# A written-out opening in another order: blocks 0, 8 and 12 loaded ahead of the first weight slab, single roots for blocks 0 and 4, and the second chunk's first unit in token halves

## The chip, the core and the metric

The kernel runs on one core of one Trainium2 chip. The core has TensorE (PE, matmuls; its weight loads are shown as PEld), VectorE (DVE), ScalarE (ACT), GpSimd (POOL) and a sync engine (SP) that issues the DMAs. The metric is the device time of one execution in microseconds; less is better. A profiled execution gives a span (first to last instruction) and the start and length of every instruction in it. Times inside the program are us from the span's start.

## What is computed

```python
xn = _layernorm(x)                                   # x: 2048 tokens x 448, float32
A  = irfft2(rfft2(xn) * (w_r + 1j * w_i))            # a filter in the frequency domain
g  = xn @ W_gate; u = xn @ W_up                      # 448 -> 1792
B  = (where(g > 0, g, 0) * u) @ W_down               # 1792 -> 448
return x + A + B
```

Every matrix product is made from float16 halves (a high part and the rest) so that float32 accuracy is kept: three matmuls in place of one.

## The kernel before

The 2048 tokens are 16 *blocks* of 128 tokens. Four blocks form a *chunk*: chunk 0 has blocks 0, 4, 8 and 12, the next one in the work's order, chunk 2, has blocks 2, 6, 10 and 14. A block is loaded, its mean and variance taken, normalized, split into a high and a low half (tile `tt`), and transposed; the transposed chunk is the tile `T` (512 token columns, 128 for each block). In the opening, chunk 0 is transposed by TensorE through PSUM and copied out; chunk 2 by DMA transposes from SP.

The gate and up weights come as 14 *slabs* (`W0` to `W13`), each with a gate half `g0` and an up half `g1` of 256 KB. The scale of a half comes from its squares (ACT), a sum over all partitions (POOL) and two bit steps on DVE; then its high half is made by one pass (ACT) and its low half by another (DVE). A *unit* is one slab on one chunk: ten matmuls per half into a PSUM bank, with some closing matmuls on half the rows (line L764), and then ACT and DVE passes (relu, product, split). After five slabs the down product of the group begins (line L834). The spectral part runs on DVE and in between on TensorE.

All engines run their instructions in program order. For the body a planner sets that order from costs. The opening, up to the first units of chunk 2, is instead a list of piece names, `OPENING`, read from left to right: each name issues its instructions at that place on each engine, so two pieces of different engines keep only their own engine's order. The names used here:

- `lxN`, `lyN`: load block N for normalizing, for the residual. The packet `lx4` is larger: it also holds the 128x128 identity that TensorE's transposes need as their second operand.
- `stN`: statistics of a block (BN_STATS and BN_AGGR on DVE). `sqA`, `rsA` (B, C): reciprocal root on ACT and four small DVE steps, for two or four blocks at once. In the change also `sqN`, `rsN`, `nmN` for one block, the last step (bias) apart.
- `xnN` on DVE, `axN` on ACT: the normalized block in float32. `hiN` on ACT from the input, `hxN` on ACT from the normalized block, `vhN` on DVE: its high half. `loN` (DVE): its low half. `cpN` (POOL): two small copies.
- `tpAN`, `tpBN`: three and five TensorE transposes of a block. `vevAN`, `aevAN` (and B): their copy out of PSUM by DVE or by ACT.
- `lw`: the next weight half; `lwdF`: a down slab. `wsqWFgG` squares, `parWF` POOL's sum, `wscWF` scale, `whiWFgG` the high half on ACT (`vwWFgG`: on DVE), `wloWFgG` the low half on DVE.
- `warm`, `kwN`, `warmN`: matmuls without a result, on a zeroed tile (line L1098).
- `hhGH`, `lhGH`, `hlGH`: slab 0's matmuls on chunk 0, for half G of the weights and token half H (256 columns). `ahGH`, `bhGH`, `chGH`: the same for slab 1. `hqGB`, `lqGB`, `kqGB`: on a single block B (0: block 0, 1: block 4).
- `guFgG`: a later slab on chunk 0; `hpF`: closing matmuls; `gzFgG`: slab F on chunk 2; `gyFgGhH`, `gxFgGhH`: the same on token half H. `re`, `tm`, `gh`, `gl` (`rz`, `tz`, `hz`, `lz`): the passes behind a unit. `dmN`: DMA transpose of a block. `n0`: four small copies of rows of chunk 0. `lfd`: load of the table `fd_t`.

SP's loads use eight semaphores in turn, so a load is issued only when the one eight places ahead has landed. The weight buffer `wst` has eight places.

Of the kernel before, what the change touches and what calls it, by code (L numbers as in the profile page):

```python
# [10 lines left out]
F32 = mybir.dt.float32  # L11
# [22 lines left out]
tpB12 wsqW3g0 vevB8 wloW1g0 ah10 wsqW3g1 vevB12 ah01 parW2 ah11 lwd2 wloW1g1 wscW2 bh00 hl11 hl01 lx14 whiW2g0
bh01 hp0 ch10 whiW2g1 lw st2 bh11 st6 re0 wloW2g0 bh10 wsqW4g1 ch00 ch11 tm0 gu2g0 parW3 wscW3 st14 wsqW4g0
whiW3g0 wloW2g1 ch01 ly0 parW4 wscW4 whiW3g1 wloW3g1 lw wsqW5g1 lx10 whiW4g0 wloW3g0 gh0 re1 st10 gu2g1 tm1 hp2
sqC rsC wsqW5g0 xn6 gu3g0 re2 parW5 wscW5 whiW5g0 tm2 wloW4g0 xn10 xn14 hx14 lwd4 hx6 lo6 hi10 whiW5g1 lo10
gu4g0 hx2 wloW5g0 whiW4g1 cp14 xn2 wdq0 gl0 cp10 gu3g1 wloW4g1 lo14 lwd3 wdq4 wdq2 cp2 re3 tm3 cp6 wloW5g1 gh1
gu4g1 gh2 wdq3 ly12 lo2 hp4 wdq1 wdp wdsc wdh4 dm10 gl1 re4 ly8 wdh3 gl2 gu5g1 tm4 gh4 dm14 gl4 dm6 gu5g0 dm2
re5 lfd gz0g0 wdl3 gz0g1 tm5 hp6 gh3 gl3 rz0 gh5 wdl4 gl5 wdh1 wdl1 wdh2 wdl2 n0 wdh0 wdl0 gz1g0 tz0 gz1g1 rz1  # L40
hz0 tz1 hz1 lz0 lz1
"""
# [102 lines left out]
def tile_gfnet_reglu(ctx: ExitStack, tc: tile.TileContext, x, xr, xi, wgu, wd, wf, c_fd, c_fm, c_im, c_row, c_id,  # L145
# [104 lines left out]
    mv = {}  # L250

    def ln_stats(q, j):
        n2 = q + 4 * j
        st = ft([128, 6], F32, "bst", 2)
        V.bn_stats(st, xr_t[n2])
        if j == 0:
            mv[q] = ft([128, 4, 2], F32, "mv", 2)
        V.bn_aggr(mv[q][:, j, :], st)

    rst = {}  # L260

    def ln_sd(q, js=(0, 1, 2, 3)):
        w = ft([128, 4, 4], F32, "rs", 3)
        n = len(js)
        rst[q, js[0]] = w[:, :, 0:n], mv[q][:, js[0]:js[-1] + 1, :]
        A.activation(w[:, 0, 0:n], rst[q, js[0]][1][:, :, 1], AF.Abs_reciprocal_sqrt, bias=eps)

    def ln_rstd(q, js=(0, 1, 2, 3), bias=False):
        w, m = rst[q, js[0]]
        r0, t, r, nm = (w[:, i] for i in range(4))  # L270
        V.scalar_tensor_tensor(t, m[:, :, 1], 1e-5, r0, op0=OP.add, op1=OP.mult)
        V.scalar_tensor_tensor(t, t, -0.5 * 2048, r0, op0=OP.mult, op1=OP.mult)
# [25 lines left out]

    def ln_hi(n2, fused=False):
        new_tt(n2)  # L300
        o = tt[n2].rearrange("p a b -> p (a b)")[:, 0:D]
        r, nm, _ = rst[n2 % 4, n2 // 4]
        if fused:
            A.activation(o, xr_t[n2], AF.Identity, scale=r, bias=nm)  # L304
        else:
            A.activation(o, xn[n2], AF.Copy)
# [789 lines left out]
    def keep_warm(n):  # L1096
        for _ in range(n):
            P.matmul(wps, warm[:, 0:128], warm, start=True, stop=True)  # L1098

    pieces = {"lfd": lambda: nc.sync.dma_start(fd_t, c_fd),  # L1100
              "lw": load_wn, "warm": lambda: keep_warm(NWARM),
              **{f"kw{n}": (lambda n=n: keep_warm(n)) for n in (1, 3, 4)},
              "wdp": lambda: wd_sum(len(groups[0])),
# [5 lines left out]
    for c, q in enumerate(CHUNKS[:2]):  # L1109
# [14 lines left out]
    def gu_slab(f, g, q=CHUNKS[0]):  # L1124
# [16 lines left out]
    for f in groups[0] + [ahead[2]]:  # L1141
# [149 lines left out]
```

## Time and profile before

| | us |
|---|---|
| median of 3 runs | 442.76 |
| lowest, highest | 442.59, 443.61 |
| the profiled execution, its own time | 443.54 |
| its span, first to last instruction | 441.8 |
| TensorE busy in that span | 435.3 |
| DVE, ACT, POOL busy | 382.4, 184.6, 29.0 |
| first matmul with weights starts | 11.21 |
| first unit on chunk 2 starts | 41.60 |
| first down matmul starts | 50.89 |

In a row of the timeline stand the start, the length, engine, line, operation, the tiles (written <- read), the size and the count, and in brackets the idle time of the engine just before and what ended it. In a group row there is the count, then busy us and mean ns of one, then the idle time before. A row of waits names who waited for whom, the sum in us, the count, and the longest. SPq and PEld queue rows are the issuing side.

### The profile page before, as it was taken

The page shows a single profiled execution, that of the slowest core. Times are in us where ns is not written, and L with a number is a line of the kernel's source. Part 1 is how long each engine was busy: PE and PEld are TensorE (multiplying, and loading weights), DVE is VectorE, ACT ScalarE, POOL GpSimd, SP SyncE. Part 2 cuts the span into 40 slices and gives each one's busy share as a digit, 9 for nine tenths or more (in the row PEclk, how much of TensorE's full clock was granted, in tenths as well). Part 3 has the DMA queues.
Part 4 walks back from the last instruction along what each step waited for, and adds up shares of the span by engine and source line. Part 5 has one row for each costly group of instructions (what it writes and reads, how often), then busy time and mean ns, then how long its engine had stood idle before and what let it go on. Part 6 is the DMA issues. An engine that isn't in the chain of part 4 may idle for free.

```text
span 441.8 us, 7428 instructions
## 1 busy us (share of the span) xinstructions
PE 435.3 (99%) x2641; PEld 221.5 (50%) x2641; DVE 382.4 (87%) x957; ACT 184.6 (42%) x396; POOL 29.0 (7%) x75
## 2 busy tenths in 40 slices
PE   8999999999999999999999999999999999999997
PEld 3743454454555544444545444444545556555664
DVE  6998677788996879999999999988997989798644
ACT  5995454274557327144023358233213232244220
POOL 3230020011100040000000020000000000000000
PEclk9999999999999999999999999999999999999999
DMA  7929899004021124242220210001111121210212
GB/s 244 322 75 213 267 357 216 23 1 97 23 86 58 45 68 129 84 127 85 85 85 1 84 42 2 0 1 42 43 43 49 48 98 30 74 56 33 77 63 104
DMA packets 37612, 39.54 MB, mean 90 GB/s; under 512 B 16534, under 2 KB 33352, under 8 KB 37576
## 3 DMA queue, kind: packets, MB, share of 16 engines
q1 hardware_dynamic: 37576, 39.09, 29.3%
q8 instruction: 20, 0.33, 0.3%
q14 instruction: 16, 0.13, 0.1%
HBM read 24.38 MB, written 3.67 MB: 64 GB/s over the span
## 4 chain that ended last, share of the span: by engine, by line
PE 90%; ACT 3%; DVE 2%; DMA 2%; issue 1%; SPq 1%; POOL 0%; ACTq 0%
PE bank L757 49%; PE bank L834 27%; PE bank L764 3%; PE fx L648 2%; PE fx L369 2%; PE fx L667 2%; PE fx L406 2%; PE bank L853 2%; DMA y<-in_xr 1%; DMA T<-tt 1%; ACT wt L699 1%; ACT junk L185 1%; ACT tt L304 1%; DVE wt L703 1%; DVE g L803 0%
## 5 line engine op out<-in xcount | busy, mean ns | idle before, releaser
L757 PE MATMUL bank<-T,wt 128*128 128x512 f16 (+1 forms) x1160 | 253.2, 372 | 1.8 <-DMA T<-tt 1.1
L757 PEld LDWEIGHTS <-wt 128*128 128x128 f16 x1160 | 110.9, 98 | 128.4 <-issue 7.2
L834 PE MATMUL bank<-wdt,h 128*128 128x448 f16 x624 | 122.6, 352 | 0.0
L834 PEld LDWEIGHTS <-h 128*128 128x128 f16 x624 | 60.6, 98 | 55.4
L807 ACT ACTIVATE h<-g 128x512 f16<-128x512 f32 x56 | 35.0, 627 | 77.2 <-DVE g L803 77.2
L799 ACT ACTIVATE g<-bank 128x512 f32<-128x512 f32 x56 | 33.2, 592 | 79.9 <-PE bank L757 43.8
L803 DVE SCALAR_TENSOR_TENSOR g<-bank,g 128x512 f32<-128x512 f32 x56 | 38.4, 685 | 10.8 <-PE bank L757 7.0
L811 DVE TENSOR_TENSOR h<-g,h 128x512 f16<-128x512 f32 x56 | 38.4, 686 | 10.3 <-ACT h L807 10.2
L840 DVE SCALAR_TENSOR_TENSOR xy<-bank,dsc,xy 128x448 f32<-128x448 f32 x44 | 29.9, 679 | 3.2 <-PE bank L834 2.9
L632 ACT ACTIVATE vt<-y,fsc 128x456 f16<-128x456 f32 x15 | 10.1, 674 | 34.5 <-issue 14.0
L699 ACT ACTIVATE wt<-wst,wsc 128x512 f16<-128x512 f32 x28 | 19.3, 714 | 11.7 <-DVE wsc L195 10.0
L703 DVE SCALAR_TENSOR_TENSOR wt<-wst,wsc,wt 128x512 f16<-128x512 f32 x28 | 20.4, 743 | 0.5 <-ACT wt L699 0.5
L188 POOL PARTITION_ALL_REDUCE wm<-wm x15 | 10.3, 686 | 152.1 <-ACT junk L185 117.6
L672 DVE SCALAR_TENSOR_TENSOR xy<-fx,fsc,xy 128x448 f32<-128x448 f32 x16 | 10.8, 681 | 10.9 <-PE fx L667 10.9
L185 ACT ACTIVATE junk<-wst 128x512 bf16<-128x512 f32 x28 | 17.2, 616 | 0.0
L764 PE MATMUL bank<-T,wt 64*128 64x512 f16 x112 | 15.6, 380 | 0.0
L397 ACT ACTIVATE Xh<-X 128x456 f16<-128x456 f32 x16 | 9.3, 579 | 13.0 <-DVE X L395 8.3
L648 PE MATMUL fx<-im,vt 128*128 128x128 f16 x192 | 13.3, 219 | 0.0
L667 PEld LDWEIGHTS <-pgh 114*128 114x128 f16 x192 | 10.9, 98 | 3.8 <-issue 0.8
L406 PE MATMUL fx<-Xh,fm 128*128 128x456 f16 x48 | 12.7, 356 | 0.0
L648 PEld LDWEIGHTS <-vt 128*128 128x128 f16 x192 | 11.6, 98 | 1.3
L667 PE MATMUL fx<-idc_t,pgh 114*128 114x112 f16 x192 | 12.1, 213 | 0.0
(168 smaller groups left out, 478.3 us busy)
## 6 DMA issues: line engine op xcount, KB each, us to landing
wst<-in_wgu SPq DMA_DIRECT2D x28, 256.0 KB
sw<-y SPq DMA_DIRECT2D x56, 112.2 KB
wf<-in_wf SPq DMA_DIRECT2D x16, 228.0 KB
xy<-in_x SPq DMA_DIRECT2D x16, 224.0 KB
y<-in_xr SPq DMA_DIRECT2D x15, 224.0 KB
out<-xy SPq DMA_DIRECT2D x15, 224.0 KB
wdst<-in_wd SPq DMA_DIRECT2D x14, 224.0 KB
fm<-in_c_fm SPq DMA_DIRECT2D x4, 256.0 KB
```

The lines of the kernel that those rows point to most:

```text
L648: P.matmul(o, v[:, h, w], m[:, c, :], start=(i == 0), stop=(i == 2), skip_group_check=True)
L667: P.matmul(ps[:, o], h[:, a, i, :], idc_t[:, b, o], start=(j == 0), stop=(j == 2), skip_group_check=True)
L699: A.activation(w[:, 0:4, :], wst[f, g], AF.Copy, scale=wsc[f, g])
L703: V.scalar_tensor_tensor(w[:, 4:8, :], st, sc, w[:, 0:4, :], op0=OP.mult, op1=OP.subtract)
L757: last["P"] = P.matmul(hps[f, q][g][:, cs], wt[f, g][:, a, :], Tq[q][:, b, cs], start=(start and i == 0), stop=(stop and i == len(seq) - 1 ...
L764: m = P.matmul(hps[f, q][g][:, 0:512], wt[f, g][rows, 7, :], Tq[q][rows, b, :], start=start, stop=stop).ins
L799: last["A"] = A.activation(g1s[f, q], hps[f, q][0], AF.Relu, scale=2.0 ** -22).ins
L803: last["V"] = V.scalar_tensor_tensor(g1, hps[f, q][1], 2.0 ** -22, g1, op0=OP.mult, op1=OP.mult).ins
L807: A.activation(ht[f, q][:, 0, :], g1s[f, q], AF.Copy)
L811: V.tensor_tensor(h[:, 1, :], g1s.pop((f, q)), h[:, 0, :], op=OP.subtract)
L834: last["P"] = P.matmul(ps[:, 0:D], ht[f, q][:, a, js], wdt[f][:, b, :], start=(i == 0), stop=(i == n - 1)).ins
L840: last["V"] = V.scalar_tensor_tensor(xy[:, n2, :], dps[n2][:, 0:D], dsc[:, g:g + 1], xy[:, n2, :], op0=OP.mult, op1=OP.add).ins
```

## The change

Nothing of what is computed changes. The order in `OPENING` is another, and new pieces let some work be cut or placed differently:

- Loads: blocks 0, 8 and 12 first, then slab 0's two halves, then the packet of block 4 with the identity as the sixth load; it was the second. Down slabs 4, 3 and 2 and the table `fd_t` are loaded earlier than before.
- Block 0 has a root of its own (`sq0 rs0 nm0`), block 4 too (`sq4 rs4`, the bias step `nm4` at the end of the opening); blocks 8 and 12 share one. Block 0 is normalized by ACT (`ax0 hx0`), the high halves of 12 and 4 are made by DVE (`vh12 vh4`), and 4 is normalized by DVE (`xn4`), 8 and 12 by ACT.
- Six of chunk 0's eight copies out of PSUM go from DVE to ACT; slab 0's up half is made by DVE (`vwW0g1`).
- Warm-up: 14, 4 and 1 matmuls in place of 21 and 4.
- Slab 0 on chunk 0 is cut into blocks 0 and 4 (128 columns each) and the half with 8 and 12, so that it can start with block 0.
- Slab 0 on chunk 2 (`gz0g0 gz0g1`) is cut into token halves (`gy0g0h0 gy0g1h0`, then `gx0g0h1 gx0g1h1`). The DMA transposes go in the order 6, 2, 10, 14; it was 10, 14, 6, 2. `n0` stands ahead of them.

```diff
-NWARM = 21
-OPENING = """lx0 st0 lx4 st4 sqA rsA ax4 hi0 lx8 st8 lx12 xn0 lw cp0 lw lw lw hx4 warm tpA4 st12 tpA0 lo0 lx6 sqB rsB cp4 lo4
...
-re5 lfd gz0g0 wdl3 gz0g1 tm5 hp6 gh3 gl3 rz0 gh5 wdl4 gl5 wdh1 wdl1 wdh2 wdl2 n0 wdh0 wdl0 gz1g0 tz0 gz1g1 rz1
+OPENING = """lx0 lx8 lx12 st0 sq0 rs0 lw nm0 warm14 warm4 ax0 lw hx0 lx4 cp0 st8 st12 sqB tpA0 lo0 wsqW0g0 parW0g0 lw wsqW0g1 rsB
...
+wloW5g0 cp10 cp14 wdq3 xn14 wdp gu4g1 lo14 gl1 hp4 gu5g1 wdsc re4 dm10 tm4 dm14 gh2 gu5g0 gh3 wdh0 gy0g0h0 gy0g1h0 gl2
...
     def ln_sd(q, js=(0, 1, 2, 3)):
-        w = ft([128, 4, 4], F32, "rs", 3)
+        w = ft([128, 4, 4], F32, "rs", 4)
...
+    def ln_bias(q, js):
+        w, m = rsb[q, js[0]]
+        V.scalar_tensor_tensor(w[:, 3], m[:, :, 0], -1.0, w[:, 2], op0=OP.mult, op1=OP.mult)
...
-    def ln_hi(n2, fused=False):
+    def ln_hi(n2, fused=False, eng=None):
...
+        if eng is not None:
+            eng.tensor_scalar(o, xr_t[n2], mean, r, op0=OP.subtract, op1=OP.mult)
...
-    def w_hi(f, g):
+    def w_hi(f, g, eng=None):
...
+            eng.tensor_scalar(w[:, 0:4, :], wst[f, g], wsc[f, g], None, op0=OP.mult)
...
+    def gz_half(g, h, first):
+        if g == 0 and first:
+            gu_open(0, CHUNKS[1])
+        gu_full(0, CHUNKS[1], (g,), half[h], first, False)
+
+    for g in range(2):
+        for h in range(2):
+            piece(f"gy0g{g}h{h}", gz_half, g, h, True)
+            piece(f"gx0g{g}h{h}", gz_half, g, h, False)
...
+                for j in range(2):
+                    for tag, sq in (("hq", seq1[0:3]), ("lq", seq1[3:6]), ("kq", seq2)):
+                        piece(f"{tag}{g}{j}", gu_full, f, q, (g,), slice(128 * j, 128 * j + 128), tag == "hq" and j == 0,
+                              False, sq)
```

What the list makes of the engines' order is shown at three places. First SP's loads at the very start, before (`in_xr` is a block, `in_xi` the packet of block 4 with the identity, `in_wgu` a weight half, `in_wd` a down slab):

```order
L225 DMA y_66<-in_xr 128x448
L220 DMA g_127<-in_xi 128x512
L225 DMA y_68<-in_xr 128x448
L225 DMA y_69<-in_xr 128x448
L231 DMA wst<-in_wgu 128x512 x4
```

and now:

```order
L224 DMA y_66<-in_xr 128x448
L224 DMA y_67<-in_xr 128x448
L224 DMA y_68<-in_xr 128x448
L230 DMA wst<-in_wgu 128x512 x2
L219 DMA g_159<-in_xi 128x512
L230 DMA wst<-in_wgu 128x512
L240 DMA wdst<-in_wd 128x448
```

The packet with the identity went from the second to the sixth place, and a down slab came ahead of the second half of slab 1.

Second, DVE in the stretch that ends at the first real matmul. `mv` and `rs` are the statistics and the root, `eg` and `wsc` the scale of slab 0, `T` the copy out of PSUM, `wt` a weight half. Before:

```order
L322 TENSOR_TENSOR tt_101<-y_67,tt_101 128x64
L191 TENSOR_SCALAR eg<-wm 128x1
L195 TENSOR_SCALAR wsc<-eg 128x1
L345 COPY T_62<-fx 128x3x128
L191 TENSOR_SCALAR eg<-wm 128x1
L195 TENSOR_SCALAR wsc<-eg 128x1
L345 COPY T_62<-fx 128x3x128
L345 COPY T_62<-fx 128x5x128 x2
L703 SCALAR_TENSOR_TENSOR wt<-wst,wsc,wt 128x512 x2
```

and now, from block 12's high half on (`g_159` is block 4):

```order
L307 TENSOR_SCALAR tt_101<-y_68,mv,rs 128x448
L254 BN_STATS bst<-g_159 128x6
L257 BN_AGGR mv<-bst 128x2
L190 TENSOR_SCALAR eg<-wm 128x1
L194 TENSOR_SCALAR wsc<-eg 128x1
L190 TENSOR_SCALAR eg<-wm 128x1
L194 TENSOR_SCALAR wsc<-eg 128x1
L270 SCALAR_TENSOR_TENSOR rs<-mv,rs 128x1
L271 SCALAR_TENSOR_TENSOR rs<-rs 128x1
L272 SCALAR_TENSOR_TENSOR rs<-rs 128x1
L707 TENSOR_SCALAR wt<-wst,wsc 128x512
L350 COPY T_62<-fx 128x5x128
```

The copies out of PSUM that stood here are on ACT, and block 4's statistics and root steps stand ahead of the pass that makes slab 0's up half.

Third, SP around chunk 2's transposes (`T2`), with the numbers of the buffers. Before:

```order
L330 DMA_TRANSPOSE T2_63<-tt2_102 128x8x128
L214 DMA xy_61<-in_x 128x448
L330 DMA_TRANSPOSE T2_63<-tt0_100 128x8x128
L330 DMA_TRANSPOSE T2_63<-tt1_101 128x8x128
L330 DMA_TRANSPOSE T2_63<-tt3_103 128x8x128
L231 DMA wst_750<-in_wgu 128x512
```

and now:

```order
L356 DMA Tl0_96<-T0_62 16x512 x3
L357 DMA Tl0_96<-T0_62 64x512
L335 DMA_TRANSPOSE T2_63<-tt0_100 128x8x128
L335 DMA_TRANSPOSE T2_63<-tt1_101 128x8x128
L335 DMA_TRANSPOSE T2_63<-tt2_102 128x8x128
L335 DMA_TRANSPOSE T2_63<-tt3_103 128x8x128
```

The four small copies of chunk 0 came ahead of the transposes, and the load between the first and the second transpose is gone.

More of the change, by code (lines that the diff above doesn't have):

```diff
@@ L34 @@
[L34 to L38, printed above, removed]
@@ L39 @@
-gu4g1 gh2 wdq3 ly12 lo2 hp4 wdq1 wdp wdsc wdh4 dm10 gl1 re4 ly8 wdh3 gl2 gu5g1 tm4 gh4 dm14 gl4 dm6 gu5g0 dm2
-re5 lfd gz0g0 wdl3 gz0g1 tm5 hp6 gh3 gl3 rz0 gh5 wdl4 gl5 wdh1 wdl1 wdh2 wdl2 n0 wdh0 wdl0 gz1g0 tz0 gz1g1 rz1
-hz0 tz1 hz1 lz0 lz1
+OPENING = """lx0 lx8 lx12 st0 sq0 rs0 lw nm0 warm14 warm4 ax0 lw hx0 lx4 cp0 st8 st12 sqB tpA0 lo0 wsqW0g0 parW0g0 lw wsqW0g1 rsB
+lwd4 vh12 tpB0 hi8 lx2 lw lw st4 tpA12 aevA0 lfd sq4 wscW0g0 tpA8 parW0g1 wscW0g1 rs4 aevA8 vwW0g1 warm1 whiW0g0 vevB0
+lwd3 lx6 vh4 hq10 cp12 aevA12 wsqW1g1 wsqW1g0 parW1 hq00 hh01 kq00 tpA4 aevA4 cp4 kq10 hh11 wloW0g1 wloW0g0 lq10 lw
@@ L42 @@
+hi10 wloW4g0 whiW5g1 whiW4g1 lo10 lwd1 gu4g0 cp2 hx14 re3 n0 wloW5g1 wloW4g1 whiW5g0 tm3 wdq4 wdq2 gh1 wdq1 dm6 dm2
+wloW5g0 cp10 cp14 wdq3 xn14 wdp gu4g1 lo14 gl1 hp4 gu5g1 wdsc re4 dm10 tm4 dm14 gh2 gu5g0 gh3 wdh0 gy0g0h0 gy0g1h0 gl2
+gh4 re5 gx0g0h1 gx0g1h1 wdh2 tm5 wdh3 hp6 wdl3 wdh1 gz1g0 nm4 ly0 wdh4 gh5 gz1g1 gl3 wdl1 rz0 gl4 tz0 wdl0 hz0 wdl4
+rz1 lz0 wdl2 tz1 hz1 gl5 lz1
 """
@@ L255, in ln_stats @@
         V.bn_stats(st, xr_t[n2])
-        if j == 0:
+        if q not in mv:
             mv[q] = ft([128, 4, 2], F32, "mv", 2)
         V.bn_aggr(mv[q][:, j, :], st)
-    rst = {}
+    rst, rsb = {}, {}
     def ln_sd(q, js=(0, 1, 2, 3)):
-        w = ft([128, 4, 4], F32, "rs", 3)
+        w = ft([128, 4, 4], F32, "rs", 4)
         n = len(js)
-        rst[q, js[0]] = w[:, :, 0:n], mv[q][:, js[0]:js[-1] + 1, :]
-        A.activation(w[:, 0, 0:n], rst[q, js[0]][1][:, :, 1], AF.Abs_reciprocal_sqrt, bias=eps)
+        rsb[q, js[0]] = w[:, :, 0:n], mv[q][:, js[0]:js[-1] + 1, :]
+        A.activation(w[:, 0, 0:n], rsb[q, js[0]][1][:, :, 1], AF.Abs_reciprocal_sqrt, bias=eps)
     def ln_rstd(q, js=(0, 1, 2, 3), bias=False):
-        w, m = rst[q, js[0]]
+        w, m = rsb[q, js[0]]
         r0, t, r, nm = (w[:, i] for i in range(4))
@@ L695, in w_scale @@
             wsc[f, k] = sc[:, i:i + 1]
-    def w_hi(f, g):
+    def w_hi(f, g, eng=None):
         w = wt[f, g] = mt([128, 8, 128], F16, "wt", 2 * NR + 4)
-        A.activation(w[:, 0:4, :], wst[f, g], AF.Copy, scale=wsc[f, g])
+        if eng is None:
+            A.activation(w[:, 0:4, :], wst[f, g], AF.Copy, scale=wsc[f, g])
+        else:
+            eng.tensor_scalar(w[:, 0:4, :], wst[f, g], wsc[f, g], None, op0=OP.mult)
     def w_lo(f, g):
@@ L1100, in tile_gfnet_reglu @@
     pieces = {"lfd": lambda: nc.sync.dma_start(fd_t, c_fd),
-              "lw": load_wn, "warm": lambda: keep_warm(NWARM),
-              **{f"kw{n}": (lambda n=n: keep_warm(n)) for n in (1, 3, 4)},
+              "lw": load_wn, **{f"warm{n}": (lambda n=n: keep_warm(n)) for n in range(1, 25)},
               "wdp": lambda: wd_sum(len(groups[0])),
@@ L1155, in tile_gfnet_reglu @@
             piece(f"whiW{f}g{g}", w_hi, f, g)
+            piece(f"vwW{f}g{g}", w_hi, f, g, V)
             piece(f"wloW{f}g{g}", w_lo, f, g)
```

21 lines of the change are left out of this document (14 added, 7 removed).

## The prediction

> **What bounds the kernel now.** I read the page's busy times first, then TensorE's waits, then the timeline of the opening engine by engine, then the chain that ended last.
>
> ```profile
> PE 435.3 (99%) x2641; PEld 221.5 (50%) x2641; DVE 382.4 (87%) x957; ACT 184.6 (42%) x396; POOL 29.0 (7%) x75
> PE bank L757 <- DMA T<-tt: 1.1, 1, 1.1
> 41.00:441.80 400.80, 397.09 (x2412) 201.53 (x2412) 347.93 (x853) 152.23 (x325) 18.04 (x40) 1.00 0.26 78
> ```
>
> TensorE is busy for 435.3 of 441.8 us, and its one long wait behind the start is for a DMA; the last row (stretch, PE busy, PEld, DVE, ACT, POOL, clock, DMA share, GB/s) leaves 3.7 us idle after 41 us, of which 0.6 ends the transpose wait and the rest is the final store. So the kernel is a fixed string of matmuls: the moment at which TensorE passes a given matmul in the opening moves the end by the same amount, as long as no new wait comes up behind it.
>
> ```profile
> 1.23 6.71 PE L1098 MATMUL bank<-row_t 128*128 128x512 f16 x21 [1.23 <-DVE row_t L1170]
> 9.07 1.03 PE L1098 MATMUL bank<-row_t 128*128 128x512 f16 x4
> 11.21 0.49 PE L757 MATMUL bank<-T,wt 128*128 128x256 f16 x3 [0.71 <-DVE T L345]
> 15.29 0.45 PE L337 MATMUL bank<-g,tt 128*128 128x128 f16 x5
> 15.57 0.49 PE L757 MATMUL bank<-T,wt 128*128 128x256 f16 x3
> 15.90 0.44 PE L337 MATMUL fx<-g,tt 128*128 128x128 f16 x5
> 41.60 3.63 PE L757 MATMUL bank<-T,wt 128*128 128x512 f16 x16 [1.09 <-DMA T<-tt]
> 50.89 0.73 PE L834 MATMUL bank<-wdt,h 128*128 128x448 f16 x3
> ```
>
> Until 11.21 TensorE does nothing of the result except transposes: 25 matmuls (lines L1098) are warm-up. What holds that start is the loads and what is made of them. The 1.09 us before 41.60 is the first unit on the second chunk waiting for the last of four DMA transposes.
>
> ```profile
> 2.13 5.27 DMA y<-in_xr
> 8.05 0.37 SPq L231 DMA_DIRECT2D wst<-in_wgu  x1
> 8.69 0.33 SPq L231 DMA_DIRECT2D wst<-in_wgu  x1
> 10.15 0.33 SPq L231 DMA_DIRECT2D wst<-in_wgu  x1
> 36.71 4.84 DMA T<-tt
> ```
>
> The first row is of the chain: the fourth load (block 12) landed at 7.40. SP keeps eight loads in flight, so its issues at 8.05, 8.69 and 10.15, the 13th, 14th and 16th, mark the landings of loads five, six and eight. I take these as landings by place in the queue, since what is loaded has nearly the same size (224 to 256 KB).
>
> **Warm-up and the first matmul.** Six warm-up matmuls of 25 go. They are worth nothing: they fill a time that other work sets. The new path to the first real matmul runs through the input packet of block 4, which also holds the identity. It was load two and is load six, so it lands at 8.69, and no transpose can run before. TensorE's 18 warm-ups end about 0.6 us earlier than the 21 did (7.9 to 7.3), so it waits some 1.4 us there.
>
> ```profile
> 3.26 0.63 DVE L255 BATCH_NORM_STATS2 bst<-y 128x6 f32<-128x448 f32 x1 [2.09 <-DMA y<-in_xr]
> 3.92 0.18 DVE L258 BATCH_NORM_AGGREGATE mv<-bst 128x2 f32<-128x6 f32 x1
> 4.87 0.29 ACT L266 ACTIVATE rs<-mv,eps 128x2 f32<-128x2 f32 x1 [2.63 <-DVE mv L258]
> 5.20 0.16 DVE L271 SCALAR_TENSOR_TENSOR rs<-mv,rs 128x2 f32<-128x2 f32 x1 [0.36 <-ACT rs L266]
> 5.39 0.16 DVE L272 SCALAR_TENSOR_TENSOR rs<-rs 128x2 f32<-128x2 f32 x1
> 9.12 0.61 ACT L185 ACTIVATE junk<-wst 128x512 bf16<-128x512 f32 x1
> 9.73 0.75 ACT L304 ACTIVATE tt<-y,rs 128x448 f16<-128x448 f32 x1
> L297 DVE TENSOR_SCALAR y<-y,mv,rs 128x448 f32<-128x448 f32 x6 | 3.0, 506 | 0.0
> L703 DVE SCALAR_TENSOR_TENSOR wt<-wst,wsc,wt 128x512 f16<-128x512 f32 x12 | 8.7, 740 | 0.0
> L345 DVE COPY T<-fx 128x384 f16<-128x384 f16 x3 | 1.0, 350 | 0.0
> L799 ACT ACTIVATE g<-bank 128x512 f32<-128x512 f32 x6 | 3.5, 581 | 0.3 <-PE bank L764 0.3
> 10.00:20.00 10.00, 9.29 (x91) 7.32 (x91) 9.45 (x29) 9.25 (x21) 2.86 (x8) 1.00 0.95 340
> ```
>
> The first matmul now takes the up half of slab 0 (vwW0g1, moved from ACT to DVE). DVE: block 4's statistics at 8.71, 0.84 as at 3.26 to 4.10, so 9.55. ACT meanwhile: slab 0's two squares at 7.45 and 8.06 (loads four and five), hi8 at 8.67, the eviction aevA0 at 9.35, then block 4's root. That ACT eviction of 384 columns is not in the trace: it is bounded by DVE's copy, 0.35, and by ACT's 512 columns out of PSUM, 0.58; I take 0.48, nearer the ACT row, since it is the same engine. The root starts at 9.75 and ends at 10.04; three DVE steps 0.19 apart put vwW0g1 at about 10.55. Its time lies between 0.51 (448 columns, one scalar pass) and 0.74 (512 columns, two operands); I take 0.56, the first scaled to 512 columns. So 11.11, and the matmul at 11.15, against 11.21: -0.06. The gate half (ACT, from 10.34, 0.71) is ready as early. Bounds of these two durations: -0.25 to +0.25.
>
> Block 0's own root frees its normalization earlier (one block's statistics instead of two ahead of the root, some 0.75 us), but its transposes then stand before the identity, so this gain is hidden. DVE's net load falls: six of eight evictions (four of 0.35, two of 0.48) go to ACT, against three small steps, vwW0g1 and one more 0.5 pass, some -0.7 us. ACT takes up about 3 us and gives off some passes; it has little room, being busy for 9.25 of the 10 us from 10 to 20 (last row, fifth figure).
>
> **First to second chunk.** TensorE needed 29.30 us from 11.21 to 40.51 (41.60 less 1.09). Two more transposes fall after the first matmul, 56 ns each (15.29 to 15.57 for five): +0.11. Slab 0 on blocks 0 and 4 runs as 40 matmuls of 128 columns in place of 20 of 256: 2 x 56 against 110 ns (15.57 to 15.90 for three), +0.04. The Trainium skill, "TensorE: Matmul & The Clock Gate", section "Back-to-back issue gap", puts a sustained pair of weight load and 128-column matmul at some 81 ns; by it these 40 would cost 1.0 us more and the sum below would end at 442.6. The rows of the transposes, which are such pairs, show 56, so the trace disagrees, and the sum goes by them.
>
> Short waits inside this stretch depend on DVE's low halves of weights; TensorE's sequencer shows one:
>
> ```profile
> PEld L764 <- DVE wt L703: 0.5, 1, 0.5
> ```
>
> With DVE relieved I take 0.2 off; the bounds are -0.5 (all gone) and +0.5 (ACT's evictions 0.12 to 0.15 longer each and late in turn). So the second chunk is reached at 11.15 + 29.30 + 0.15 - 0.2 = 40.40.
>
> **The wait at 41.60.** The unit's 40 matmuls of 256 columns replace 20 of 512, at the same columns: 20 x 2 ns = +0.04. Its first 20 need only blocks 2 and 6, its second 20, from 42.6, blocks 10 and 14.
>
> ```profile
> 31.09 1.36 SPq L330 DMA_TRANSPOSE T<-tt  x1
> 34.00 3.96 SPq L330 DMA_TRANSPOSE T<-tt  x3
> SPq L330 <- DVE tt L322: 9.8, 1, 9.8
> 43.49 1.87 SPq L351 DMA_DIRECT2D Tl<-T  x3
> 45.41 0.59 SPq L352 DMA_DIRECT2D Tl<-T  x1
> ```
>
> The first block of this chunk could go at 31.09; with 6 and 2 first, both are issued by some 34 and, at the slowest landing shown (4.84 behind an issue), are there by 39. Blocks 10 and 14 are issued by about 38, as the fourth was, and land by 41.6 at the latest; 42.6 is asked. So the 1.09 goes: -1.09. The four small copies of n0 now stand on SP ahead of the transposes: they cost some 2.5 us of issue, covered by SP's 9.8 us of waiting there. Nobody in this stretch reads what the earlier loads of the table fd_t and of down weights bring, but they put off slabs and blocks in SP's queue: a rival below. Block 4's bias step (nm4), moved to the end of the opening, has no reader before.
>
> **Sum.** -0.06 + 0.15 - 0.2 + 0.04 - 1.09 = -1.16. The profiled execution took 443.54 with a span of 441.8, 0.8 above the median of the runs; the difference applied to the median 442.76 gives **441.6**.
>
> **Rivals.**
> *Loads behind DVE (the other side).* On DVE the statistics of block 14 now stand ahead of slab 2's low half, and its load is number 22. From 10.15 (eighth) another 14 loads, 3.4 MB, at the rate here:
>
> ```profile
> 11.00:12.00 1.00, 0.79 (x8) 0.66 (x9) 1.00 (x4) 1.00 (x3) 0.00 (x0) 1.00 1.05 395
> 18.49 1.22 SPq L225 DMA_DIRECT2D y<-in_xr  x1
> ```
>
> 395 GB/s lands it at 18.8. DVE gets there at 19.6: from 11.05 it has two evictions (0.8), four low halves of weights (2.65), three of blocks (1.85), two passes of 448 columns (0.85), two statistics (1.5) and two pairs of scale steps with a wait (0.9). If the buffers hold SP back as at 18.49, where a load was issued 1.2 us late, it lands later, and every us beyond 19.6 delays slab 2 and TensorE by a us. From 20.8 on the change is a loss; at 22.5 it is 442.76 - 1.16 + 2.9 = 444.5.
>
> *The clock drops.* Weight loads of the warm-up stood 0.42 us apart at first, 0.2 later:
>
> ```profile
> 4.62 0.15 PEld L1098 LDWEIGHTS <-row_t 128*128 128x128 f16 x1 [0.28 <-issue]
> 5.04 0.15 PEld L1098 LDWEIGHTS <-row_t 128*128 128x128 f16 x1 [0.28 <-issue]
> 5.40 2.04 PEld L1098 LDWEIGHTS <-row_t 128*128 128x128 f16 x10 [0.21 <-issue]
> ```
>
> So TensorE ran at half speed from 1.23 to 5.40, though the granted clock reads 1.00. Between 7.3 and 11.15 it now works for only 1.0 us (14 transposes and one warm-up), with two waits of 1.4 and 1.3 us; before it worked 2.3 us in as much time (0.6 of warm-up, 16 transposes, four warm-ups), and a wait of 0.71 us changed nothing. If half speed came back for another 4.2 us from 11.15, it would cost 2.1: 443.7. The same page, section "What's actually happening", lets the clock fall after an idle window of about 3.4 us; by that rule neither wait suffices and this rival fails, while its section on queue cycling tells of a clock that swings from short idles. No run here shows either.
>
> *The wait stays.* If blocks 10 and 14 land after 43.7, or 2 and 6 after 41.5, nothing is gained but the small terms: 442.7.
>
> *More gained.* All hidden waits vanish and vwW0g1 is short: 441.0.
>
> **How the numbers follow.** My forecast has 0.66, from 441.1 to 442.2, about half of it under 441.43; the wait stays 0.10; the clock 0.10 (of it 0.03 above 444.09); the loads 0.08 (0.05 above); more gained 0.06. A measurement of this kernel can tell about 0.3%, 1.33 us, from no change. That makes faster 0.38, same 0.54, slower 0.08. The range 440.9 to 443.4 leaves out the loads' case, a part of the clock's, and little else.
>
> **What would show it.** Right: the identity's load ends a TensorE wait of over 1 us near 8.7, the first 128-column matmul starts near 11.15, no wait on T<-tt near 40.4, and the first L834 row starts 1.2 us earlier than at 50.89. Wrong: 128-column matmuls of one row 80 or 110 ns apart; DVE waiting for y<-in_xr near 19.6; a wait on wt in TensorE after 20 us.

## The result, and the profile after

The changed kernel takes 444.87 us (median of 6 runs, 444.25 to 446.31), the kernel before 442.63 in the same session (6 runs, 441.96 to 443.61). The ratio is 1.0052, 95% interval 1.0039 to 1.0065: 0.5% slower. 441.6 was forecast, with a range that ended at 443.4; the sign was wrong too. The longest of the six, 446.31, is the only one with a granted clock of 0.996; the other five have 1.000 and end at 445.03.

The opening came out much as forecast. First the page (span, busy time, and the chain that ended last by engine) and the waits of TensorE, then its timeline:

```profile
span 443.2 us, 7501 instructions
PE 434.5 (98%) x2675; PEld 223.8 (51%) x2675; DVE 381.7 (86%) x957; ACT 185.7 (42%) x401; POOL 28.6 (6%) x75
PE 75%; DVE 16%; DMA 3%; ACT 2%; issue 2%; POOL 1%; SPq 1%; DVEq 0%; POOLq 0%; ACTq 0%
PE fx L342 <- DMA g<-in_xi: 1.2, 1, 1.2
PE bank L765 <- ACT wt L705: 1.0, 1, 1.0
PE bank L772 <- DVE g L811: 0.9, 3, 0.5
```

```profile
8.74 1.02 PE L342 MATMUL fx<-g,tt 128*128 128x128 f16 x11 [1.18 <-DMA g<-in_xi]
11.48 1.08 PE L765 MATMUL bank<-T,wt 128*128 128x128 f16 x13 [0.98 <-ACT wt L705]
36.60 8.86 PE L765 MATMUL bank<-T,wt 128*128 128x512 f16 x60
50.26 2.06 PE L842 MATMUL bank<-wdt,h 128*128 128x448 f16 x10
```

The identity's load ends a wait of 1.18 us, the first real matmul starts at 11.48, the second chunk follows the first without a gap (60 matmuls in a row), and the first down matmul is at 50.26 against 50.89. Up to there the changed kernel is 0.63 us ahead of the one profile that I had. Yet it ends later. The signs that the prediction named for being wrong don't tell it: the 128-column matmuls are 56 ns apart, DVE has no wait for a block near 19.6, and the one wait on `wt` behind 20 us (a weight load, 0.4) is no longer than that of the kernel before (0.5). New is the last row of the waits: three times a closing matmul (L772; L764 before) waits for DVE's product pass (L811). DVE now holds 16% of the chain.

A second profile of each kernel shows what really happened. Kernel before, second profile: span, and three rows of TensorE's timeline:

```profile
span 440.3 us, 7428 instructions
11.09 0.49 PE L757 MATMUL bank<-T,wt 128*128 128x256 f16 x3 [0.45 <-DVE T L345]
35.82 8.81 PE L757 MATMUL bank<-T,wt 128*128 128x512 f16 x40
49.42 0.73 PE L834 MATMUL bank<-wdt,h 128*128 128x448 f16 x3
```

The 40 matmuls from 35.82 run from the first chunk into the second without a gap. The wait of 1.09 us for the transposes, which the change was priced by, is not there. The changed kernel, second profile:

```profile
span 442.7 us, 7501 instructions
11.03 1.10 PE L765 MATMUL bank<-T,wt 128*128 128x128 f16 x13 [1.19 <-ACT wt L705]
36.15 8.86 PE L765 MATMUL bank<-T,wt 128*128 128x512 f16 x60
49.80 2.43 PE L842 MATMUL bank<-wdt,h 128*128 128x448 f16 x12
201.89 0.82 PE L772 MATMUL bank<-T,wt 64*128 64x512 f16 x6 [0.42 <-DVE g L811]
227.47 0.82 PE L772 MATMUL bank<-T,wt 64*128 64x512 f16 x6 [0.16 <-DVE g L811]
253.17 0.82 PE L772 MATMUL bank<-T,wt 64*128 64x512 f16 x6 [0.46 <-DVE g L811]
```

These two executions took 442.08 and 444.52. Their difference of 2.44 (the medians differ by 2.24) falls into the steps of the forecast like this (DVE's last pass starts at 437.26 and 438.89, rows below; the spans are read to 0.1 us):

| step | forecast | second profiles |
|---|---|---|
| start of the first real matmul | -0.06 | 11.03 - 11.09 = -0.06 |
| from it to the first down matmul | -1.10 | 38.77 - 38.33 = +0.44 |
| from there to the start of DVE's last pass | 0 | 389.09 - 387.84 = +1.25 |
| from there to the end of the span | 0 | 3.81 - 3.04 = +0.77 |
| around the span | 0 | 1.82 - 1.78 = +0.04 |
| sum | -1.16 | +2.44 |

Three things are to be explained: a gain that was not there, a loss in the body, which the change does not touch, and a loss behind the last matmul.

### The profile page after: what moved, and what is told of

It is laid out like the page before. It is cut to its first block, busy times and chain, and to the rows that moved or that the text cites. A ratio compares the mean times of both kernels' runs of the same rounds, so it can differ in the third digit from the quotient of the medians.

```text
span 443.2 us, 7501 instructions
## 1 busy us (share of the span) xinstructions
PE 434.5 (98%) x2675; PEld 223.8 (51%) x2675; DVE 381.7 (86%) x957; ACT 185.7 (42%) x401; POOL 28.6 (6%) x75
## 4 chain that ended last, share of the span: by engine, by line
PE 75%; DVE 16%; DMA 3%; ACT 2%; issue 2%; POOL 1%; SPq 1%; DVEq 0%; POOLq 0%; ACTq 0%
PE bank L765 42%; PE bank L842 19%; PE bank L772 3%; PE fx L653 2%; PE fx L374 2%; PE fx L672 2%; PE fx L411 2%; PE bank L861 2%; DVE g L811 1%; DMA y<-in_xr 1%; DVE h L819 1%; DVE xy L848 1%; DVE y L526 1%; DVE y L444 1%; POOL sw L507 1%
## 5 line engine op out<-in xcount | busy, mean ns | idle before, releaser
L765 PE MATMUL bank<-T,wt 128*128 128x512 f16 (+2 forms) x1200 | 252.7, 365 | 1.1 <-ACT wt L705 1.0
L765 PEld LDWEIGHTS <-wt 128*128 128x128 f16 x1200 | 113.4, 98 | 126.1 <-issue 6.8
L811 DVE SCALAR_TENSOR_TENSOR g<-bank,g 128x512 f32<-128x512 f32 x56 | 38.4, 685 | 12.8 <-PE bank L765 6.3
L705 ACT ACTIVATE wt<-wst,wsc 128x512 f16<-128x512 f32 x27 | 18.7, 712 | 10.2 <-DVE wsc L194 10.2
L772 PE MATMUL bank<-T,wt 64*128 64x512 f16 x112 | 15.6, 379 | 0.9 <-DVE g L811 0.9
L405 DVE TENSOR_TENSOR Xh<-X,Xh 128x456 f16<-128x456 f32 x16 | 10.0, 625 | 4.2 <-ACT Xh L402 4.2
```

The costliest lines, as they stand in the source:

```text
L765: last["P"] = P.matmul(hps[f, q][g][:, cs], wt[f, g][:, a, :], Tq[q][:, b, cs], start=(start and i == 0), stop=(stop and i == len(seq) - 1 ...
L772: m = P.matmul(hps[f, q][g][:, 0:512], wt[f, g][rows, 7, :], Tq[q][rows, b, :], start=start, stop=stop).ins
L811: last["V"] = V.scalar_tensor_tensor(g1, hps[f, q][1], 2.0 ** -22, g1, op0=OP.mult, op1=OP.mult).ins
```

## Experiments

The body's order on each engine is set by the planner and the scheduler from simulated times, so a changed opening also gives another body. To take the two apart, every instruction traced behind the opening (3746 in both kernels) was tied to its predecessor on its engine by an order edge without a wait, in a recorded order:

```diff
+    for e, runs in BODY.items():      # BODY: for each engine, the places of its instructions in issue order
+        seq = [n for r in runs.split() for n in range(int(r.split("-")[0]), int(r.split("-")[-1]) + 1)]
+        body = [i for i in tc.nc.cur_bb.bb.instructions
+                if str(i.engine).split(".")[-1] == e and "Boundary" not in type(i).__name__][-len(seq):]
+        for m, n in zip(seq, seq[1:]):
+            tc.add_manual_dep(body[n], body[m].name, NOSYNC, reason="order of the body")
```

Below, "own order" means the body's order in the changed kernel, "old order" that of the kernel before. Each ratio is to runs of the kernel before on the same chip (medians there 442.11, 442.47, 442.50 and 442.61 in the four sessions). In each run's record stands the granted clock, a mean over the run; where runs are told apart below, it is by that. Two terms come back: the *body's time*, from the start of the first down matmul to the start of DVE's last pass (387.84 us in the second profile of the kernel before), and the *tail*, from there to the end of the span.

**New opening, old order.**

> The changed opening, word for word, with the body behind it (everything traced after the opening, 3746 instructions) held to the issue order that it has in the kernel before, on all five engines, by order edges alone. Theory BODY (the loss comes from the other order that the scheduler gave the body, above all DVE's, which is late at three closings): the opening's gain stays, so about 1 us faster than before, 441.3 to 442.0, and no wait of the closing half matmuls on DVE's g pass at 202, 228 and 253 us. Theory OPENING (the opening itself leaves something late that the body pays for, whatever its order): 444.4 to 445.2, as the changed kernel. Theory NOISE (the profiled pair misleads, and the chip's store at the end is it): 443.5 to 444.5, with no wait in the body and a late last store.

443.73 (5 runs, 443.07 to 443.96), ratio 1.0032 (1.0020 to 1.0043). The three waits on DVE are gone; from the first down matmul to the last, the trace stays at the same distance from the kernel before (1.29 us), so the body's time is 387.84 again. So theory BODY holds for these waits, but it missed the time: the opening alone is slower than before, and the forecast gain isn't in it. NOISE had about this time, but with a late last store, which this profile doesn't have. Three of the five runs have a clock of 0.995 (443.73 to 443.96). The rows show why the profiled one, which is one of them, is so late:

```profile
core 0: 441.9 us, clock 0.995
1.23 5.46 PE L1106 MATMUL bank<-row_t 128*128 128x512 f16 x18 [1.23 <-DVE row_t L1195]
8.21 0.78 PE L342 MATMUL fx<-g,tt 128*128 128x128 f16 x11 [1.53 <-DMA g<-in_xi]
8.94 0.34 PE L342 MATMUL bank<-g,tt 128*128 128x128 f16 x3
9.11 0.38 PE L1106 MATMUL bank<-row_t 128*128 128x512 f16 x1
10.60 1.64 PE L765 MATMUL bank<-T,wt 128*128 128x128 f16 x13 [1.11 <-DVE wt L707]
12.03 0.53 PE L342 MATMUL fx<-g,tt 128*128 128x128 f16 x3
12.35 3.99 PE L765 MATMUL bank<-T,wt 128*128 128x128 f16 x37
```

The first real matmul is early, at 10.60. But the groups of 13, 3 and 37 that follow take 1.64, 0.53 and 3.99 us. In the changed kernel's second profile the same 13 and 37 took 1.10 and 3.30 (11.03 and 12.13), and three transposes take 0.33. TensorE ran at half speed in part of them: its matmuls start 107 ns apart for 128 columns (56 else) from 10.97 to 14.36, a stretch of 3.4 us with a granted clock of 0.50. The mean of 0.995 shows it too: 3.4 us here and 0.9 us behind the last matmul were at half speed. The two runs at 0.999 and 1.000 still took 443.07 and 443.20, about 1.0 over the kernel before; what they owe that to was not profiled.

**Old opening, own order.**

> The opening of the kernel before, with the body held to the issue order that it has in the changed kernel. Theory BODY: slower than before by what the body lost, 1.1 us of waits shown in the trace of the changed kernel and perhaps up to 3: 443.7 to 445.7. Theory OPENING: 442.4 to 442.9, as before. Theory NOISE: 442.4 to 443.0.

444.04 (6 runs, 443.56 to 445.92), ratio 1.0049 (1.0033 to 1.0064). So the body's other order alone costs as much as the whole change, on an opening that is the old one word for word. In the profile the body's time is 389.63, that is +1.79; the tail is the old one (3.0). The waits of TensorE and DVE:

```profile
PE bank L764 <- DVE g L803: 1.6, 3, 1.0
DVE y L553 <- DMA sw<-y: 1.6, 2, 1.4
DVE yx L553 <- DMA sw<-yx: 0.9, 1, 0.9
```

DVE waits 2.5 us for the *swaps* of the spectral part (tile `sw`: SP copies a half spectrum with the two halves of its partitions exchanged, DVE adds it in a *pair* step), and afterwards comes late to three product passes. In the kernel before, second profile, the same waits are shorter, and no matmul waits for a product pass:

```profile
DVE y L553 <- DMA sw<-y: 0.7, 1, 0.7
DVE yx L553 <- DMA sw<-yx: 0.2, 1, 0.2
```

In all five profiles of the own order the one for `yx` is 0.9.

**The kernel before and the changed one, second profiles.**

> The kernel before, unchanged, for a second profile. The first profiled execution was 0.9 us above the median of its runs. Theory TYPICAL: the wait of TensorE for T<-tt near 41.6 us is again 1.0 to 1.2 us. Theory UNTYPICAL: that wait is shorter (0.2 to 0.6), TensorE's first down matmul starts that much before 50.89, and the time is 442 to 442.7; then a part of the gain that was predicted was never to be had.

> The changed kernel, unchanged, for a second profile. Theory BODY: the three waits of closing half matmuls on DVE's g pass (0.9 us by the page) come again at the same places, and the time is 444.3 to 445.3. Theory NOISE: they are gone or elsewhere. The last piece of the output, whose sixteenth part landed 1 us behind the others in the first profile, lands with them if that was chance.

442.08 and 444.52, shown above. UNTYPICAL holds for the kernel before, and by more than it said: the wait is not shorter but gone. The waits of the changed one came again, in the same three places. The late step of the last store came again too (below). A third profile of the kernel before:

> The kernel before, unchanged, for a third profile. Theory CHANCE: no wait for T<-tt, the second chunk's unit follows without a gap near 40.2, span 440.1 to 441.4. Theory of the prediction: a wait of 1 us there.

442.42, span 440.6, no wait for T<-tt. Of the seven profiles that were taken with the old opening, or with other numbers of warm-ups in it, one shows that wait: the one from which the forecast was made.

**Warm-ups back.** In the opening of the first experiment, with three warm-ups more at each of the two places (six in all, where the expectation says seven):

```diff
-... warm14 warm4 ax0 ... vwW0g1 warm1 whiW0g0 ...
+... warm14 warm7 ax0 ... vwW0g1 warm4 whiW0g0 ...
```

> The changed opening with the body held to the order before, as in the first experiment, and the seven warm-up matmuls put back (21 ahead of the first transposes and four ahead of the first real matmul, in place of 18 and one). Theory CLOCK (in the first experiment's profile TensorE's matmuls ran at half speed from 10.97 to 14.36, behind a stretch of 3.4 us that it worked only 1.4 us of, and that cost 1.3 us): with the warm-ups back no such stretch, 0.9 to 1.3 us faster than the first experiment, 0.0 to 0.5 over the kernel before, and 128-column matmuls 56 ns apart throughout. Theory OPENING (the new order of loads and evictions is itself slower): still 1.2 to 1.8 over the kernel before.

442.75 (11 runs, 442.34 to 443.18), ratio 1.0005 (0.9996 to 1.0013): 1 us less than the first experiment, and no longer distinct from the kernel before. No run has a granted clock under 0.998, and the profile has no stretch at half speed behind 11 us. That is what CLOCK expected; that the clock is all that the warm-ups brought back isn't shown, since the first experiment's two runs at full clock were late as well. What is left of the new opening is neither gain nor loss.

**Fewer warm-ups in the old opening.** To see this without the new opening, the kernel before with the same six warm-ups taken out:

```diff
-NWARM = 21
+NWARM = 18
-... tpB0 kw4 tpB4 ...
+... tpB0 kw1 tpB4 ...
```

> The kernel before with the change's six warm-up matmuls fewer (18 and one in place of 21 and four), body in its order of before. Theory CLOCK (a stretch of 3.4 us with TensorE mostly idle ahead of the first matmul sets the clock to half for the next 3.4): some runs show a granted clock of 0.995 to 0.996 and are 1.0 to 1.7 us longer than the others, which stand within 0.3 of the kernel before; none of the runs of the kernel before shows such a clock. Theory of the prediction (the warm-ups are worth nothing): all runs within 0.3 us of the kernel before, clock 0.998 or more.

442.18 (12 runs, 441.90 to 443.90), ratio 1.0001 (0.9989 to 1.0012): the same as the kernel before, but in two groups. 5 of 12 runs have a granted clock of 0.995 or 0.996 and take 443.36 to 443.90; the other seven have 0.999 or 1.000 and take 441.90 to 442.18. The step is 1.45 us between the medians (443.46, 442.01). None of the 92 runs of the kernel before in the four sessions has a clock under 0.999. So CLOCK holds for the two groups, but the faster group is 0.5 under the kernel before (442.50), more than the 0.3 that was allowed: what the five lose, the seven nearly make up, and the mean of the 12 (442.69) is 0.1 over that of the kernel before (442.59). Which group matters was tried apart (`NWARM` 18 with `kw4`, and 21 with `kw1`):

> The kernel before with 18 warm-up matmuls ahead of the transposes in place of 21, and the later four kept; body in its order of before. Theory LATE GROUP (the stretch of 3.4 us that goes wrong is the one just ahead of the first real matmul, and the late four are in it): no run at a clock under 0.998, and all at 441.9 to 442.3, up to 0.5 us under the median of the kernel before, since the first group no longer runs into the transposes when it starts at half speed for long. Theory EARLY GROUP: some runs at 0.995 to 0.996 and 1.3 to 1.6 us longer, as with 18 and one.

> The kernel before with the 21 kept and one in place of the later four; body in its order of before. Theory LATE GROUP: some runs at 0.995 to 0.996 and 1.3 to 1.6 us longer than the others. Theory EARLY GROUP: none, and all within 0.3 us of the kernel before.

18 and four: 442.56 (11 runs), ratio 0.9995 (0.9986 to 1.0005), no run under 0.999. 21 and one: 442.62 (11 runs), ratio 1.0005 (0.9994 to 1.0016), two runs at 0.995, 443.39 and 443.71. This points to the later group, on two runs of eleven against none. The loss can't be read here, since three runs at full clock are as late (443.25 to 443.66). The profiled one of them owes 0.43 us to a late swap, though its body is in the old order (body's time 388.27):

```profile
PE bank L764 <- DVE g L803: 1.0, 2, 0.7
DVE y L553 <- DMA sw<-y: 1.4, 1, 1.4
```

That 18 would also start earlier and gain 0.5 didn't show. Over all kernels that had one warm-up in the later place, 16 of 48 runs had a clock of 0.994 to 0.996; over the variants with four there, 3 of 73. These counts bear out the later group, across different openings and orders.

**Halves alone.** In the old opening, with the transposes in their old order, the half of blocks 10 and 14 first:

```diff
-... gz0g0 wdl3 gz0g1 ...
+... gy0g0h1 gy0g1h1 gx0g0h0 gx0g1h0 wdl3 ...
```

> The kernel before with one part of the change alone: the first unit on the second chunk in token halves (the half of blocks 10 and 14, whose transposes go first there, ahead of the other), the body held to its order of before. Theory CHANCE (the wait for the transposes stood in one of two profiles of the kernel before, and in no typical execution): within 0.2 us of the kernel before; no run above its median by 1 us. Theory of the prediction (the wait is there in every execution and the halves remove it): 0.9 to 1.1 us faster.

442.53 (12 runs), ratio 1.0002 (0.9990 to 1.0013). The halves by themselves change nothing, as CHANCE has it. It also said that no run would be 1 us above the median, and three are, at 443.64 to 444.04 (the kernel before goes up to 444.06 in that session). The profiled one is among them. It has no wait at the second chunk; it has the body's waits, in the old order:

```profile
PE bank L764 <- DVE g L803: 1.6, 3, 0.6
185.56 0.40 DVE L553 TENSOR_TENSOR y<-y,sw 128x228 f32<-128x228 f32 x1 [2.31 <-DMA sw<-y]
```

Here a single swap came 2.3 us late for DVE, 0.67 in the second profile of the kernel before at the same instruction (183.29 us). The body's time is 389.05, +1.21. So the old order has some slack for late swaps, but not for every one; why a swap is late in one execution and not in another stays open.

**DVE relieved in the own order.** The passes of the forward pair step made shorter; this leaves out three quarters of that step, so only the time counts:

```diff
-        V.tensor_tensor(u[:, :, 0], u[:, :, 0], t[:, :, 1], op=o1)
-        V.tensor_tensor(u[:, :, 1], u[:, :, 1], t[:, :, 0], op=o2)
+        n = 1 if sgn > 0 else 4
+        V.tensor_tensor(u[:, 0:n, 0], u[:, 0:n, 0], t[:, 0:n, 1], op=o1)
+        V.tensor_tensor(u[:, 0:n, 1], u[:, 0:n, 1], t[:, 0:n, 0], op=o2)
```

> The changed kernel, body held to its own order, with the two passes of each forward pair step (DVE adds the swapped half-spectrum; 16 steps, 32 passes of 228 columns, 0.39 us each) cut to 57 columns: it leaves out three quarters of that step and so relieves DVE by about 0.2 us a pass, some 2 us ahead of 200 us, without moving an instruction. Theory DVE LATE (in that order DVE waits longer for the swaps near 175 and 189 us, comes late to three g passes, and TensorE's closings wait for it): the three waits near 202, 228 and 253 us are gone and the time is 1.0 to 1.3 us under the changed kernel's: 443.2 to 443.9, where the granted clock is 1.00. Theory ORDER ON TENSORE (the matmuls' own order costs it): as the changed kernel, 444.3 to 445.0.

443.81 (7 runs, 443.07 to 444.47), ratio 1.0029 (1.0018 to 1.0040). The page's chain, the swap waits of DVE and the one pass that waits longest:

```profile
PE 96%; DMA 1%; ACT 1%; DVE 0%; SPq 0%; issue 0%; POOL 0%; ACTq 0%
DVE y L559 <- DMA sw<-y: 1.3, 2, 1.0
DVE yx L559 <- DMA sw<-yx: 0.9, 1, 0.9
188.78 0.22 DVE L559 TENSOR_TENSOR y<-y,sw 128x57 f32<-128x57 f32 x1 [1.03 <-DMA sw<-y]
```

The swaps are as late as in the changed kernel, no instruction has moved, but DVE does each pass in 0.22 in place of 0.40, and TensorE waits for its product passes nowhere: DVE's share of the chain falls from 16 to 0%. The first down matmul starts at 50.27 and DVE's last pass at 438.11 (row below), so the body's time is 387.84, to the hundredth that of the kernel before, in the own order. DVE LATE holds, and the matmuls' own order by itself costs nothing. The time is about 1 us under the changed kernel's, inside what was expected.

**Eight more instructions on DVE.** Own order, with tiny memsets at the start:

```diff
+        pad = mt([128, 1], F32, "pad")
+        for _ in range(8):
+            V.memset(pad, 0.0)
```

> The changed kernel, body held to its own order, with eight more tiny memsets on DVE at the start, where DVE waits for the first load. Theory FETCH (in both profiles of the changed kernel the last step of the last store came 0.8 to 1.0 us behind the other 15, while 8 KB of DVE's instructions were read at 440.4 to 440.7; eight instructions more move that read to an earlier place): the last store lands with all its steps, and the time is 0.6 to 1.0 us under the changed kernel's, that is 1.2 to 1.8 over the kernel before. Theory CHANCE: as the changed kernel, 2.2 to 2.5 over the kernel before, or the late step comes and goes without the read.

444.86 (6 runs), ratio 1.0044 (1.0028 to 1.0060), but four of the six ran at a clock of 0.996 (444.81 to 445.06), as this kernel has one warm-up in the sensitive place. The two others took 443.17 and 443.50, against 444.25 to 445.03 of the changed kernel at full clock; that is 0.7 and 1.0 over the kernel before of the session, less than FETCH expected. The tail, by DVE's last pass in four kernels: before (second profile), changed (second profile), this one, and the one with short pairs:

```profile
437.26 0.33 DVE L857 SCALAR_TENSOR_TENSOR xy<-fx,dsc,xy 128x112 f32<-128x112 f32 x1
```
```profile
438.89 0.33 DVE L865 SCALAR_TENSOR_TENSOR xy<-fx,dsc,xy 128x112 f32<-128x112 f32 x1
```
```profile
440.03 0.33 DVE L865 SCALAR_TENSOR_TENSOR xy<-fx,dsc,xy 128x112 f32<-128x112 f32 x1
```
```profile
438.11 0.33 DVE L866 SCALAR_TENSOR_TENSOR xy<-fx,dsc,xy 128x112 f32<-128x112 f32 x1
```

With spans of 440.3, 442.7, 443.1 and 442.0 the end comes 3.04, 3.81, 3.07 and 3.89 us behind the start of that pass. The two long ones are in the new opening and the own order and have no memsets. In those two (and in the first profile of the changed kernel) the 16th step of the last store landed some 0.8 to 1.0 us behind the other 15, and a read of 8 KB of instructions falls just there. The packets by queue, from 440.2 to 441.0 in the changed kernel's second profile, then from 439.5 to 442.0 in the kernel with the memsets:

```profile
q1 hardware_dynamic: 161, 0.07, 31.1%
q14 instruction: 1, 0.01, 3.8%
```
```profile
q1 hardware_dynamic: 432, 0.46, 52.8%
```

With eight more instructions on DVE that read has moved (to 424.2) and the late step is gone. All 17 profiles agree: the three with such a read inside the last store have the late step and a tail of 3.8 to 4.0; the 14 without it have neither. Their tail is 3.0, also with the own order on the old opening, and 3.3 in the four with the new opening and the old order, which was not traced. So FETCH is borne out; that the read itself delays the step is inferred from its falling together with it in three profiles.

**Two versions meant to beat both**, on the opening with the warm-ups back and the old order: slab 0's high halves ahead of block 4's root, and the identity's packet fifth:

```diff
-... aevA0 lfd sq4 wscW0g0 tpA8 parW0g1 wscW0g1 rs4 aevA8 vwW0g1 warm4 whiW0g0 vevB0 ...
+... aevA0 lfd wscW0g0 whiW0g0 tpA8 parW0g1 wscW0g1 vwW0g1 sq4 rs4 aevA8 warm4 vevB0 ...
```
```diff
-... ax0 lw hx0 lx4 cp0 ...
+... ax0 lx4 hx0 lw cp0 ...
```

> A version meant to beat both: as the first of these (new opening, warm-ups back, body in its order of before), with slab 0's two high halves made ahead of block 4's root on both engines, since the first 20 matmuls read block 0 alone. If DVE and ACT are what the first matmul waits for: it starts at 10.4 to 10.6 instead of 11.0, and the time is 0.2 to 0.5 under the kernel before. If the moment is given back by later waits (for block 4, whose normalization is now 0.5 us later): as the first of these, 0.0 to 0.5 over the kernel before.

> A second version meant to beat both: new opening, warm-ups back, body in its order of before, with block 4's packet, which holds the identity, loaded fifth and the second half of slab 0 sixth. If the identity's landing holds the start (TensorE waited 0.6 to 1.6 us for it in every profile of the new opening): the first real matmul at 10.4 to 10.8 and 442.0 to 442.5, 0.0 to 0.4 under the kernel before. If slab 0 holds it: the first real matmul at 11.3 or later and 443.0 to 443.4.

443.21 (11 runs), ratio 1.0019 (1.0011 to 1.0028), and 443.50 (11 runs), ratio 1.0025 (1.0016 to 1.0034). Both are slower than the kernel before, and further behind than either of their expectations had them (0.7 and 1.0 us). The first starts its first real matmul at 11.06, not at 10.4 to 10.6. One row of the first and two of the second:

```profile
11.97 0.71 PE L765 MATMUL bank<-T,wt 128*128 128x256 f16 x7 [0.41 <-ACT T L348]
```
```profile
10.53 0.34 PE L342 MATMUL bank<-g,tt 128*128 128x128 f16 x3 [1.26 <-ACT tt L309]
12.07 1.09 PE L765 MATMUL bank<-T,wt 128*128 128x128 f16 x13 [0.33 <-ACT wt L705]
```

In the first the evictions pushed back on ACT are waited for next; in the second, the transposes of block 8 wait 1.26 us for its pass on ACT, and the first real matmul is late with them. A third, 18 and four warm-ups with the halves:

> 18 and four warm-ups with the second chunk's first unit in token halves, body in its order of before: a version meant to beat both. If the kernel before loses time at the second chunk in a part of its executions: no run above 442.6 and a median of 441.9 to 442.2. If the spread of the kernel before comes from its start alone: as with 18 and four without the halves.

442.68 (11 runs, 442.06 to 444.13), ratio 1.0001 (0.9991 to 1.0010), as without the halves; so nothing at the second chunk was to be gained. No version was found that beats the kernel before by more than can be told.

## Why the prediction was wrong, point by point

- **The wait at 41.60 (-1.09).** This is the term that failed first. The wait belonged to one execution: one of seven profiles of the old opening has it. Whether the halves would have removed it isn't shown, since there was none to remove. The prediction had the warning in hand: the profiled execution stood 0.8 us above the median of the runs, with a single stall of 1.1 us in it. It then subtracted that stall from the median, which, by the other six profiles, did not contain it. In the second profile the first down matmul is 1.47 us earlier (49.42 against 50.89) without any edit. The rival *the wait stays* asked only whether transposes could be late; that there might be no wait to remove was not among the rivals.
- **The first real matmul (-0.06).** Right in its steps: the identity's landing, block 4's statistics and root, and slab 0's up half on DVE, whose pass runs from 10.49 to 10.97 in the second profile (10.55 to 11.11 forecast). The row above names ACT's pass, which ends 0.02 later. That the difference is -0.06 to the hundredth is luck: in the five profiles of this opening the moment lies between 10.60 and 11.50, and in the first pair it is 11.48 against 11.21.
- **First to second chunk (+0.15 - 0.2).** The 128-column matmuls are 56 ns apart (37 with some 256-column ones between, 109 ns each, take 3.30 us), as the row of the transposes had it. So the trace bore out the row against the 81 ns of the Trainium skill, "TensorE: Matmul & The Clock Gate", section "Back-to-back issue gap". The 0.2 for relieved waits had the wrong sign: a wait of 0.27 us for slab 1's high half on ACT stands at 14.60 (PEld L765 <- ACT wt L705: 0.3, 1, 0.3). The stretch is 0.44 longer in all; 0.2 of it are the added transposes and splits that were counted, 0.27 is this wait, less 0.12 that a gap of the kernel before took at 13.6. The rest, 0.09, is the kernel before's: its stretch is 38.33 here and 38.42 in its third profile.
- **The warm-ups (0).** The reason was wrong, the size hardly mattered here. The cover that was named, the wait for the loads, hides their time; it does not hide what they hold up, the clock. The rival *the clock drops* named the mechanism and gave it 0.10, with a size of 2.1 where 1.45 was measured. But it strikes only in some executions (one of six of the changed kernel, 446.31 us at 0.996), so it is not what makes the median 444.87; and in the old opening taking out the six changed neither mean nor ratio by more than can be told. The same page of the Trainium skill, section "What's actually happening", lets the clock fall after an idle window of about 3.4 us, and the prediction concluded that by it two waits of 1.4 and 1.3 us cannot suffice. The stretches of 3.4 us agree with the trace of the first experiment; the conclusion does not, since TensorE worked in between and still fell to half speed.
- **The body (0).** Wrong, and a term that the sum didn't have. "The moment TensorE passes a given matmul in the opening moves the end by the same amount" holds to the hundredth as long as no new wait comes up behind it, as the sentence itself asks: the body's time is 387.84 in ten of the twelve profiles in the old order, and also in the own order once DVE is relieved. But the change gave the body another order, in which DVE, waiting for swaps, came late and TensorE waited for it: +1.10 and +1.25 in the two profiles of the changed kernel, +1.79 on the old opening. In the old order it happened in two of twelve profiles (+0.43 and +1.21). *Loads behind DVE* looked for a loss on DVE at 20 us; it came at 200 us.
- **The tail (0).** +0.77, not foreseen: in the trace of before no instruction read falls on the last store. Together with the body it is 2.0 us of the 3.6 between forecast and measurement; the wait that wasn't there is 1.1 of the rest.

## What to carry to other kernels

If the profiled execution lies above the median of its runs, the stall that one wants to remove may be the whole of the excess: look for it in a second profile before pricing it. Where a scheduler orders the rest of the program from simulated times, an edit at the start is also an edit everywhere behind it; compare the orders to the end, see which engine has little slack there (DVE at 87% with transfers to wait for), and hold the old order by edges if only the start is meant to change. Matmuls without a result may be worth their clock even where their time is covered.

## What the chip showed that I had not expected

- In the two profiles that show it, TensorE falls to half speed for one stretch of 3.4 us, and the stretch before need not be idle: in the first experiment TensorE worked 1.5 of the 3.9 us from the end of the warm-ups (6.69) to 10.60, and half speed began at 10.97. With four warm-ups there it works 2.2 of 3.1 us (7.97 to 11.09; 0.82, 0.34 and 1.03 from the rows of 8.54, 9.55 and 9.73) and no run of that kernel fell.
- The traces tell more about when. At the start the warm-ups go from 427 to 216 ns apart at a moment that differs from run to run (4.1 to 7.2 us). Counted from there in steps of 3.41 us, TensorE was busy for 47% of the step that ends at 10.92 in the first experiment, and for 47% of the one that ends at 10.99 in the kernel with the memsets; half speed began there in both. In the other 15 profiles no such step up to 17 us was under 53%, and none shows half speed there. By this reading the same waits are harmless or not by where the steps happen to lie. Two cases are few, and the limit between 47 and 53% is an estimate from them.
- The longest wait of DVE for a swap is 0.6 to 1.0 us in 14 of 17 profiles, 1.4 in two and 2.3 in one. In the old order 1.3 us of such waits in all cost nothing; a single one of 1.4 made TensorE wait 1.0 and the body 0.43 longer, one of 2.3 made it wait 1.6 and the body 1.21 longer.
- Where a read of 8 KB of instructions fell on the last store, the end came 0.8 to 1.0 us later; eight more instructions on one engine moved the read away.
